# Tiles 2 to 6 and their attention played from one written list, three quarters of tile 6's first layer by 7 block products

## The chip, the core and the metric

One core of a Trainium2 chip. TensorE (PE) multiplies and writes into PSUM, which this kernel uses as 8 banks of 512 float32 in each of 128 partitions. VectorE (DVE) and ScalarE (ACT) read PSUM and SBUF; GpSimd (POOL) works in SBUF; SyncE (SP) issues most DMAs. Each engine takes its own instructions in the order in which they were recorded, and waits at one whose inputs or buffers are not ready. The metric is the device time of one execution, in microseconds (us), lower is better: 273.82 us before, median of 3 runs (273.69 to 274.09).

## The reference

Linear attention on 8 batches of 8 heads, 576 positions and 64 channels, and then a two-layer network on its 4608 rows:

```python
q_s = np.exp(q - np.max(q, axis=-1, keepdims=True))
q_s = q_s / (np.sum(q_s, axis=-1, keepdims=True) + 1e-09)
k_s = np.exp(k - np.max(k, axis=2, keepdims=True))
k_s = k_s / (np.sum(k_s, axis=2, keepdims=True) + 1e-09)
kv = np.einsum('bhsd,bhse->bhde', k_s, v)
x = np.einsum('bhsd,bhde->bhse', q_s, kv)   # then (8, 576, 8, 64) -> 4608 x 512
h = x @ w_in                                # w_in 512 x 2048
g = np.maximum(0.01 * h, h)
out = g @ w_out                             # w_out 2048 x 512
```

Inputs and output are float32; the multiplications take bfloat16.

## The kernel before

The 4608 rows are 9 tiles of 512 (t = 0 to 8). A batch has 576 rows, so tile t needs batches up to the one that covers its last row: tile 3 needs batch 3, tile 7 a little of batch 7. While the network works on tile t, the attention of a later batch b is made.

**Attention of a batch.** Three loads of 1152 KB (`load_all`) bring k, q and v into a pool of 6 raw buffers (`raw_pool`, L63). For k: a tree of maxima on DVE (`k_tree`, L156), the maximum over all positions by two transposes and small reductions (`k_allmax`, L161 to L181), the subtraction (`k_sub`, L189, on DVE for batches 3 and 4, on POOL from batch 5), the exponential on ACT (`k_exp`, L197). v is cast in two halves on ACT (`v_cast`, L207). For q: maxima on DVE (`q_max`, L221), subtraction on POOL (`q_sub`, L252), exponential on ACT (`q_exp`, L260), sums and reciprocal (`q_sum`, L269, L271), normalisation (`q_norm`, L276), and a transposing DMA from SP (`q_turn`, L434). `kv` makes 72 small products (L290) into two PSUM banks, which `kd_make` (L308, L309) reads and scales on DVE. `attend_x` makes 16 products (L415) in 64-row mode into six banks and copies them to `xT` on ACT (L406).

**The network of a tile.** First layer: for each of 16 blocks of 128 hidden channels four matmuls of 512 columns into one bank (`layer1`, L469), then the activation on ACT into `gj` (`leaky`, L478). Tiles 0 to 2 have a plain second layer (L494). Tiles 3 to 6 make the second layer by 7 products instead of 8 on 2 x 2 blocks (`seven`, L813), as Strassen and Winograd do, with differences of `gj` blocks on DVE (`gsums`, L773) and sums of `w_out` blocks (`wsums`, L695). Tiles 7 and 8 (`woven`) have both layers by 7 block products, in an order written out as a list of words (`WEAVE`): the first layer is L944, with sums of `w_in` blocks (`fsums`, L875), sums of `xT` blocks (`xsums`, L892), copies to `part` buffers on ACT (L1007) and additions on DVE (L986).

PSUM is two pools: 6 banks (`psB`) for first-layer results, `pkv`, `po` and others, and 2 banks (`psO`) for second-layer results. A tile takes the bank that was given back first. `g_pool` has 5 buffers, of which a tile of rows takes 4; `osb_pool` has 3 for output rows.

**What sets the order.** For tiles 1 to 6 a loop runs over the first layer's 16 blocks and then over the second layer's products, and after step u of tile t it calls what was hooked there by `at(t, u, ...)`: `plan3`, `plan4` and `plan(b)` hook the attention of batches 3 to 7 (L616 to L658), L607 to L610 the loads, L714 the sums 3 and 4 of `w_out`, L1046 to L1050 the sums of `w_in` and of tile 7's `xT`. At the end of tile 1, for instance, `k_allmax(3)` and its two subtractions stand at step 30, ahead of the copy of that tile's last result (L488), which stands at step 31.

Of the kernel before, what the change touches and what calls it, by code (L numbers as in the profile page):

```python
# [8 lines left out]
FP32 = mybir.dt.float32  # L9
# [10 lines left out]
L = 64  # L20
# [5 lines left out]
def kernel(  # L26
# [110 lines left out]
    def k_begin(b):  # L137
        st[b]["ke"] = ke_pool.tile([P, R, HL, D], BF16, name="ke")
        st[b]["kmax"] = mx_pool.tile([P, HL, D], FP32, name="kmax")
        st[b]["kmaxT"] = mx_pool.tile([P, HL * D], FP32, name="kmaxT")  # L140
        st[b]["kall"] = mx_pool.tile([P, HL, D], FP32, name="kall")

# [295 lines left out]

    def attend_x(b, parts, engs):

        qX = st[b]["qX"].rearrange("c (r g) (h l) -> c g h r l", g=2, h=2)
        made = []
        for i in parts:
            rs = XR[i]
            n = (rs.stop - rs.start) * L
            cols = slice(b % 4 * S + rs.start * L, b % 4 * S + rs.stop * L)
            per = 512 // n
            for g0 in range(0, 2, per):
                ps = [psB_pool.tile([P, per, n], FP32, name="po", tag=BANK_TAG) for _ in range(2)]
                for gg in range(g0, g0 + per):  # L450
                    quads(
                        b,
                        gg,
                        [p[:, gg - g0] for p in ps],
                        lambda hh: qX[:, gg, hh, rs],
                        lambda o: o.rearrange("p (r l) -> p r l", l=L),
                    )
                for hp in range(2):
                    c = 2 * g0 + hp
                    made.append((xT[:, c : c + 2 * per - 1 : 2, cols], ps[hp]))  # L460
        for i, (o, p) in enumerate(made):
            move(engs[i % len(engs)], o, p)
# [146 lines left out]
    for b in range(5, B):  # L609
        at(b - 3, 20, lambda b=b: load_all(b))  # L610

    def begin_batch(b):
        k_begin(b)
        q_begin(b)

    def plan3():  # L616
        b, t = 3, 1
        at(t, 27, lambda: begin_batch(b), lambda: k_tree(b, ALLH))
        at(t, 30, lambda: k_allmax(b), lambda: k_sub(nc.vector, b, H0), lambda: k_sub(nc.vector, b, H1))
        at(t, 26, lambda: v_cast(nc.scalar, b, 0), lambda: v_cast(nc.scalar, b, 1))  # L620
        at(t, 34, lambda: q_max(b, ALLR), lambda: q_sub(nc.gpsimd, b, ALLR))
        at(t, 37, lambda: k_exp(b, ALLH))
        at(t, 45, lambda: q_exp(b, ALLR))
        at(t, 46, lambda: q_sum(b, ALLR))
        at(t, 48, lambda: q_norm(b, ALLR))
        at(t, 49, lambda: q_turn(b))
        at(t, 52, lambda: kv(b))
        at(t, 53, lambda: kd_make(b))
        at(t, 59, lambda: attend_x(b, (0, 1), (nc.scalar,)))

    def plan4():
        b, t = 4, 2
        at(t, 5, lambda: begin_batch(b), lambda: q_max(b, ALLR), lambda: q_sub(nc.gpsimd, b, ALLR))
        at(t, 17, lambda: k_tree(b, ALLH))
        at(t, 23, lambda: q_exp(b, ALLR))
        at(t, 22, lambda: k_allmax(b), lambda: k_sub(nc.vector, b, H0), lambda: k_sub(nc.vector, b, H1))
        at(t, 21, lambda: v_cast(nc.scalar, b, 0), lambda: v_cast(nc.scalar, b, 1))
        at(t, 28, lambda: q_sum(b, ALLR), lambda: k_exp(b, ALLH))
        at(t, 31, lambda: q_norm(b, ALLR))
        at(t, 31, lambda: q_turn(b))  # L640
        at(t, 34, lambda: kv(b), lambda: kd_make(b))
        hooks[t + 1, "x"] = [lambda: attend_x(b, (0, 1), (nc.scalar,))]

    def plan(b):
        t = b - 2
        at(t, 2 if b == 5 else 0, lambda: begin_batch(b), lambda: k_tree(b, ALLH))
        at(t, 16, lambda: k_allmax(b), lambda: k_sub(nc.gpsimd, b, ALLH))
        at(t, 20, lambda: q_max(b, ALLR), lambda: q_sub(nc.gpsimd, b, ALLR))
        at(t, 18, lambda: v_cast(nc.scalar, b, 0))
        at(t, 20, lambda: v_cast(nc.scalar, b, 1))  # L650
        at(t, 26, lambda: k_exp(b, ALLH))
        at(t, 32, lambda: q_exp(b, ALLR))
        at(t, 34, lambda: q_sum(b, ALLR))
        at(t, 36, lambda: q_norm(b, ALLR))
        at(t, 38, lambda: q_turn(b))
        at(t, 42, lambda: kv(b))
        at(t, 43, lambda: kd_make(b))
        hooks[t + 1, "x"] = [lambda: attend_x(b, (0, 1), (nc.scalar,))]  # L658
# [20 lines left out]
    plan4()  # L679
    for b in range(5, B):  # L680
        plan(b)
# [32 lines left out]
    at(3, 4, lambda: wsums(3), lambda: wsums(4))  # L714
# [48 lines left out]
    SEVEN, WOVEN = 3, 7  # L763
    gsum = {}

    def gsums(g_sb, kk):
        g = g_sb[kk]
        a1, a2 = g[:, 0, :, 0 : TT // 2], g[:, 0, :, TT // 2 : TT]
        b1, b2 = g[:, 1, :, 0 : TT // 2], g[:, 1, :, TT // 2 : TT]
        n = [sum_pool.tile([P, 2, TT // 2], BF16, name=f"gs{i}{kk}") for i in range(1, 5)]  # L770
        gsum[kk] = n
        for o, x, y in ((n[0], a2, b2), (n[2], a2, a1), (n[1], a1, n[0]), (n[3], b1, n[1])):
            nc.vector.tensor_tensor(out=o, in0=x, in1=y, op=ALU.subtract)  # L773

# [14 lines left out]

    def seven(t, g_sb):  # L790
        half = lambda h, c: lambda k: g_sb[k // 2][:, h, k % 2, c * HT : (c + 1) * HT]
        gs = lambda i: lambda k: gsum[k // 2][i - 1][:, k % 2]
        w = lambda h, o: w_out_sb[:, h * NK : (h + 1) * NK, o * HO : (o + 1) * HO]
        osb = [osb_pool.tile([P, 2, O], FP32, name="out_sb") for _ in range(2)]
        acc, keep = {}, {}

        def product(u, subs, x, n):
            lhs, rhs = {
                1: (half(0, 0), w(0, 0)),
                2: (half(1, 0), w(1, 0)),  # L800
                3: (gs(4), w(1, 1)),
                4: (half(1, 1), wsum[4]),
                5: (gs(1), wsum[1]),
                6: (gs(2), wsum[2]),
                7: (gs(3), w(0, 1)),
            }[n]
            first = n in (1, 2, 5)
            for i, sub in enumerate(subs):
                if first and i == 0:
                    pool, tag = (psB_pool, BANK_TAG) if x == "Y" else (psO_pool, "pout")  # L810
                    acc[x] = pool.tile([P, 2, HO], FP32, name="acc", tag=tag)
                for k in range(NK):
                    nc.tensor.matmul(  # L813
                        acc[x][:, sub],
                        lhsT=lhs(k)[:, sub * P : (sub + 1) * P],
                        rhs=rhs[:, k],
                        start=(first and k == 0 and sub == 0),
                        stop=(k == NK - 1),
                        skip_group_check=not first or sub > 0,
                    )  # L820
                run(t, u + i)

        def save(x, i):
            keep[i] = keep_tile(i)
            nc.scalar.copy(out=keep[i], in_=acc[x])  # L825

        def add(c, os, x, i):
            nc.vector.tensor_tensor(out=osb[c][:, :, os], in0=acc[x], in1=keep[i], op=ALU.add)  # L828

        def take(c, os, x):  # L830
            nc.scalar.copy(out=osb[c][:, :, os], in_=acc[x])

        product(16, both, "X", 1)
        save("X", 1)
        product(18, both, "Y", 2)
        add(0, low, "Y", 1)
        product(20, both, "X", 6)
        save("X", 6)
        run(t, "x")
        product(22, both, "Z", 5)  # L840
        save("Z", 5)
        product(24, both, "X", 7)
        add(1, high, "X", 5)
        product(26, both, "Z", 3)
        add(0, high, "Z", 6)
        put(t, osb, 0, whole)
        product(28, both, "X", 4)
        take(1, low, "X")
        put(t, osb, 1, whole)
        run(t, 30)  # L850
        run(t, 31)
# [29 lines left out]
    def xsums(t):  # L881
        home = spare_tile("xs", [P, NT - WOVEN, 4, 2, HT], BF16)
        X = {n: home[:, t - WOVEN, n - 1] for n in range(1, 5)}
        spare["X", t] = X
        B11, B12, B21, B22 = (xblock(t, c, h) for c in both for h in both)
        for o, x, y, op in (
            (X[1], B12, B11, ALU.subtract),
            (X[2], X[1], B22, ALU.add),
            (X[3], B22, B12, ALU.add),
            (X[4], B21, X[2], ALU.subtract),  # L890
        ):
            nc.vector.tensor_tensor(out=o, in0=x, in1=y, op=op)  # L892

    WEAVE = """
# [157 lines left out]
    for t in range(1, NT):  # L1052
        if t >= WOVEN:
            woven(t)
            if t == WOVEN:
                xsums(t + 1)
# [55 lines left out]
```

## Time and profile before

| what | value |
|---|---|
| median of 3 runs | 273.82 us (273.69 to 274.09) |
| the profiled execution | 273.67 us, its span 271.9 us |
| k, q, v loads of 1152 KB by SP: median from issue to landing | 6.3, 8.5, 11.1 us |
| the transposing DMA: median from issue to landing | 4.6 us |
| `gj` from a bank of 512 columns on ACT | 603 ns, 96 times |
| `gj` from a `part` buffer, copy to one, on ACT | 627, 588 ns |
| sum of bank and `part`, difference of `gj` blocks, sum of `xT` blocks, on DVE | 687, 412 to 422, 417 ns |
| k subtraction, q subtraction on POOL | 5080, 4053 ns |

The span begins with the first instruction and ends with the last; the time around it is start and end of the execution. Rows of the profile give a group's mean time for one instruction. "Busy" on PE is modelled from the starts of pipelined matmuls; the distance from one matmul's start to the next is the better measure of its rate, and a stretch of the chain of waits, divided by its number of matmuls, gives that.

### The profile page before, as it was taken

To read this page: it belongs to the slowest core of one execution; us is meant where nothing else is said; L and a number is where in the kernel's file an instruction comes from. 1 tells how busy PE (TensorE), PEld (TensorE's weight loads), DVE (VectorE), ACT (ScalarE), POOL (GpSimd) and SP (SyncE) were. 2 spreads that over 40 slices of the span, in tenths; PEclk is the share of its full clock that TensorE was granted. 3 is DMA by queue.
4 is the path that set the end of the run, shared out by engine and by line. 5 is a ranking of instruction groups with operands and counts; after the bars stand their busy time and mean duration, and the time that the engine had idled before them with its cause. 6 is when DMAs were issued, how large, how long until landed. Compare 5 with 4: busy or idle time off the path is not lost.

```text
span 271.9 us, 5971 instructions
## 1 busy us (share of the span) xinstructions
PE 262.5 (97%) x2426; PEld 174.6 (64%) x2426; DVE 214.8 (79%) x376; ACT 178.3 (66%) x315; POOL 62.9 (23%) x46
## 2 busy tenths in 40 slices
PE   8699999999999999999999999999999999999992
PEld 3267744454444444448888884478447888888882
DVE  2997888896898499999699759974499569769952
ACT  4977790578469748767685669667863479628930
POOL 2584351009004700002900290019100000000000
PEclk9999999999999999999999999999999999999999
DMA  7999996999999039999153956310622060033004
GB/s 243 336 212 368 302 199 106 381 318 389 193 244 398 29 70 300 379 208 397 43 137 75 324 214 157 62 27 0 158 50 39 1 146 11 2 79 78 0 2 154
DMA packets 37899, 46.46 MB, mean 171 GB/s; under 512 B 18160, under 2 KB 21232, under 8 KB 37872
## 3 DMA queue, kind: packets, MB, share of 16 engines
q1 hardware_dynamic: 33504, 37.82, 47.7%
q0 software_dynamic: 4048, 7.73, 12.1%
q10 hardware_dynamic: 320, 0.52, 0.6%
q8 instruction: 19, 0.31, 0.5%
q14 instruction: 8, 0.07, 0.1%
HBM read 36.70 MB, written 9.44 MB: 170 GB/s over the span
## 4 chain that ended last, share of the span: by engine, by line
PE 88%; DMA 5%; DVE 1%; issue 0%; POOL 0%; POOLq 0%
PE ph L469 34%; PE acc L813 18%; PE pout L494 14%; PE acc L965 9%; PE ph L944 9%; DMA w_in_sb<-in_moe_w_in_dram 3%; PE po L415 2%; PE pkv L290 2%; DMA qX<-qe 2%; DVE k_raw L357 1%; POOL w_in_sb L129 0%; DVE out_sb L988 0%; POOL gate L553 0%; POOLq L553 0%
## 5 line engine op out<-in xcount | busy, mean ns | idle before, releaser
L469 PE MATMUL ph<-xT,w_in_sb 128*128 128x512 bf16 (+3 forms) x576 | 99.8, 332 | 0.3 <-DMA w_in_sb<-in_moe_w_in_dram 0.3
L478 ACT ACTIVATE gj<-ph 128x512 bf16<-128x512 f32 (+2 forms) x128 | 69.9, 575 | 24.5 <-PE ph L469 21.4
L469 PEld LDWEIGHTS <-w_in_sb 128*128 128x128 bf16 x576 | 55.7, 98 | 41.1 <-issue 0.9
L494 PE MATMUL pout<-w_out_sb,gj 128*128 128x512 bf16 x192 | 43.3, 379 | 0.0
L252 POOL TENSOR_TENSOR q_raw<-q_raw,qmax 128x2304 f32<-128x2304 f32 (+3 forms) x10 | 29.7, 2975 | 40.3 <-DVE qmax L221 40.3
L494 PEld LDWEIGHTS <-gj 128*128 128x128 bf16 x192 | 18.1, 98 | 21.8 <-issue 1.1
L189 POOL TENSOR_TENSOR k_raw<-k_raw,kall 128x2304 f32<-128x2304 f32 x3 | 15.2, 5080 | 70.9 <-ACT vb L207 36.8
L269 DVE TENSOR_REDUCE qsum<-qe 128x36 f32<-128x2304 bf16 (+4 forms) x11 | 19.7, 1795 | 12.6 <-ACT qe L260 12.5
L813 PEld LDWEIGHTS <-gs 128*128 128x128 bf16 x256 | 24.7, 98 | 3.6 <-issue 0.8
L406 ACT CAST xT<-po 128x320 bf16<-128x320 f32 (+2 forms) x45 | 17.8, 493 | 10.9 <-PE po L415 10.9
L276 DVE TENSOR_TENSOR qe<-qe,qrec 128x2304 bf16<-128x2304 bf16 (+4 forms) x12 | 21.9, 1823 | 0.3
L221 DVE TENSOR_REDUCE qmax<-q_raw 128x36 f32<-128x2304 f32 (+4 forms) x11 | 19.6, 1790 | 1.6 <-DMA q_raw<-in_q_dram 1.6
L813 PEld LDWEIGHTS <-gj 128*128 128x128 bf16 x192 | 18.8, 98 | 2.8
L197 ACT ACTIVATE ke<-k_raw 128x2304 bf16<-128x2304 f32 (+2 forms) x11 | 17.6, 1600 | 3.9 <-POOL k_raw L189 3.8
L260 ACT ACTIVATE qe<-q_raw 128x2304 bf16<-128x2304 f32 (+4 forms) x11 | 16.7, 1518 | 3.9 <-DMA qX<-qe 3.1
L986 DVE TENSOR_TENSOR part_spare<-ph,part_spare 128x512 f32<-128x512 f32 x24 | 16.0, 687 | 3.4 <-PE ph L944 3.2
L1007 ACT COPY part_spare<-ph 128x512 f32<-128x512 f32 x24 | 13.1, 588 | 7.9 <-PE ph L944 7.6
L828 DVE TENSOR_TENSOR out_sb<-acc,keep 128x512 f32<-128x512 f32 x12 | 8.2, 681 | 12.1 <-ACT keep L825 7.1
L207 ACT CAST vb<-v_raw 128x1152 bf16<-128x1152 f32 x13 | 14.5, 1151 | 1.4 <-PE pkv L290 0.8
L813 PE MATMUL acc<-wsum,gs 128*128 128x256 bf16 x128 | 15.3, 273 | 0.0
L813 PE MATMUL acc<-w_out_sb,gj 128*128 128x256 bf16 x128 | 14.6, 273 | 0.0
L813 PE MATMUL acc<-w_out_sb,gs 128*128 128x256 bf16 x128 | 14.6, 273 | 0.0
(97 smaller groups left out, 347.0 us busy)
## 6 DMA issues: line engine op xcount, KB each, us to landing
out_dram<-out_sb SPq DMA_DIRECT2D x68, 128.0 KB, 2.4
k_raw<-in_k_dram SPq DMA_DIRECT2D x6, 1152.0 KB, 6.3
q_raw<-in_q_dram SPq DMA_DIRECT2D x6, 1152.0 KB, 8.5
v_raw<-in_v_dram SPq DMA_DIRECT2D x6, 1152.0 KB, 11.1
w_in_sb<-in_moe_w_in_dram POOLq DMA_DIRECT2D x4, 512.0 KB, 7.8
w_out_sb<-in_moe_w_out_dram POOLq DMA_DIRECT2D x3, 512.0 KB, 16.0
k_raw<-in_k_dram SPq DMA_DIRECT2D x2, 576.0 KB, 5.5
v_raw<-in_v_dram SPq DMA_DIRECT2D x2, 576.0 KB, 7.5
```

Of the source, the lines that this page charges most:

```text
L197: nc.scalar.activation(out=st[b]["ke"][:, :, hs].rearrange("p r h d -> p h r d"), in_=st[b]["k"][:, hs], func=AF.Exp,)
L221: nc.vector.tensor_reduce(out=m, in_=st[b]["q"][:, :, rs], axis=AX.X, op=ALU.max)
L252: eng.tensor_tensor(out=qs, in0=qs, in1=st[b]["qmax", rs.start].unsqueeze(3).to_broadcast([P, HL, n, D]), op=ALU.subtract,)
L269: nc.vector.reduce_sum(out=qsum, in_=st[b]["qe"][:, rs], axis=AX.X)
L276: nc.vector.tensor_tensor(out=qes, in0=qes, in1=st[b]["qrec", rs.start].unsqueeze(3).to_broadcast([P, n, HL, D]), op=ALU.mult,)
L406: eng.copy(out=o, in_=i)
L469: nc.tensor.matmul(ph[:, n0:n1], lhsT=w_in_sb[:, i, j * P : (j + 1) * P], rhs=xT[:, i, (c0 + n0) % NX : (c0 + n0) % NX + n1 - n0], start=( ...
L478: nc.scalar.activation(out=o, in_=ph, func=AF.Prelu, alpha=LEAKY_SLOPE)
L494: nc.tensor.matmul(pout, lhsT=g_at(g_sb, j, tsub * P, (tsub + 1) * P), rhs=w_out_sb[:, j], start=first, stop=last,)
L813: nc.tensor.matmul(acc[x][:, sub], lhsT=lhs(k)[:, sub * P : (sub + 1) * P], rhs=rhs[:, k], start=(first and k == 0 and sub == 0), stop=(k ...
L944: nc.tensor.matmul(bank[x, p][:, jj], lhsT=lhs(k, 2 * p + jj), rhs=rhs[:, k], start=(first and k == 0 and jj == 0), stop=(k == 1), skip_gr ...
L965: nc.tensor.matmul(o, lhsT=lhs(k)[:, sub * P : (sub + 1) * P], rhs=rhs[:, k], start=(first and k == 0 and (sub == 0 or x == "Z")), stop=(k ...
```

## The change

One list of words, `SCORE`, takes the place of the loop for tiles 2 to 6, of the hooks of batches 3 (from the maxima on) to 7, and of `seven` and `gsums`. Each word is recorded in the order in which it stands. A word with a digit ahead belongs to that tile: `u14` is the first layer of block 8 x 1 + 4, `l14` its activation, `P23` the fourth quarter of the plain second layer's rows 2, `P701` half 1 of block product 7 on rows 0, `n0_1` a difference of `gj` blocks, `q`, `d` and `w` the copies, the additions and the stores of results, `m7_0` block product 7 of the first layer for quarter 0, `s` and `c` its copies to and additions into `part` buffers. Others belong to a batch: `lk lq lv` loads, `kt5.0` the first step of the tree of maxima, `km ks ke` the maximum over all, the subtraction, the exponential of k, `va vb` the casts, `qm qs qe qu qn qt` the chain of q, `kv kd` the same, `A` attention products, `x` their copies. `F` is a sum of `w_in` blocks, `X` of `xT`, `T` of `w_out`; `Z` gives buffers free.

Tile 6's quarters 0 to 2 of the first layer are 21 words `m`, and quarter 3 four words `u` (blocks 6, 7, 14, 15). `F1`, `F2` and `F3` stand in tile 2's second layer, `F4` where tile 6 begins. In the built program the two buffers of the `w_in` sums are the raw buffers of v and k of batch 3, kept to the end; the loads of batches 5 to 7 go through the other four. `k_begin` no longer claims the buffer of the exponential (`k_room` does, at `ke`). Loads are single words, no longer three together. Tiles 7 and 8 keep `WEAVE`.

```diff
-    for b in range(5, B):
-        at(b - 3, 20, lambda b=b: load_all(b))
...
     def plan3():
         b, t = 3, 1
-        at(t, 27, lambda: begin_batch(b), lambda: k_tree(b, ALLH))
-        at(t, 30, lambda: k_allmax(b), lambda: k_sub(nc.vector, b, H0), lambda: k_sub(nc.vector, b, H1))
+        at(t, 27, lambda: k_begin(b), lambda: k_tree(b, ALLH))
         at(t, 26, lambda: v_cast(nc.scalar, b, 0), lambda: v_cast(nc.scalar, b, 1))
-        at(t, 34, lambda: q_max(b, ALLR), lambda: q_sub(nc.gpsimd, b, ALLR))
...
-    at(3, 4, lambda: wsums(3), lambda: wsums(4))
...
+    SCORE = """
+        2u14 km3 ks3 2u04 2l04 2u05 2l05 2u06 2u02 2l14 2l06 2u00 ksB3 ke3 2l00 2u01 2u10 2u03 2l02 2l01
+        2l03 2u11 qm3 2l11 qs3 qm4 kt4.0 qs4 kv3 kd3 2u07 2l10 2P00 2u12 qe3 qu3 qn3 2l12 T4 kt4.1 2u13 2l13
+        2u16 2l07 2l16 2u15 2l15 2u17 2l17 2P01 kt4.2 qt3 2P02 2P03 2d0 2P10 va4 F1 kt4.3 km4 ks4 F2 ksB4 F3
+        2P11 2P12 2P13 2d1 2P20 2P21 2P22 qe4 2P23 A3.0 x3.01 A3.1 A3.2 x3.00 lk5 x3.20 qu4 qn4 2P30 x3.21
+        2P31 2P32 2P33 2d2 2d3 2w0 x3.10 x3.11 kt5.0 3u00 3u11 3u10 3l00 3u04 ke4 3u01 lq5 kt5.1 3l04 3u06
...
+        3n1_1 3P100 3P101 3n3_1 lv5 3u17 3l17 3n0_3 3n1_3 3P110 3P111 3q1 A4.0 A4.1 A4.2 va5 lq6 vb5 3P500
+        x4.00 3P501 3P510 x4.01 3n3_3 3n3_2 3P600 3P601 3P511 3q5 3P610 3P611 km5 3n2_2 qm5 3P200 3P201
+        3P210 ks5 3q6 3P700 3P211 3P701 3P710 3P300 x4.11 3P301 x4.20 3d11 3P711 3d22 3P310 x4.10 qm6 2w1
+        qs5 3P311 kt6.0 x4.21 4u06 4l06 ke5 3d12 3w0 lk7 3P400 3P401 kt6.1 3P410 3P411 4u11 3q21 kt6.2 qe5
+        qu5 4u00 4l00 4l11 qn5 4u02 4l02 4u01 lv6 4l01 4u04 qt5 4l04 4u15 4u07 4u03 4l03 4u10 4l15 4l07
+        4n2_3 4n2_1 4u14 4l14 kv5 4u16 4l10 4n0_0 kd5 4u05 4l05 kt6.3 4n2_2 4u17 4l17 4u13 4u12 4P100 4n0_2
...
+        ks7 ke7 5P301 5P310 5P311 6u06 vb7 5P400 qs7 qe7 5d12 6m2_1 X6.0 Z0 6m1_0 5P401 Z1 X6.1 X6.2 X6.3
+        6m1_1 6s1_0 F4 5P410 5P411 5q21 6s1_1 6m5_2 6m1_2 6m6_0 6m5_1 qu7 6m2_0 6l06 6m6_1 6c11_0 Z2 6m5_0
+        6s1_2 6m6_2 6s6_0 6m7_0 6s5_1 6s5_0 6m3_1 6m3_0 6s6_2 6c11_1 6c22_0 6m2_2 6m4_0 6s6_1 6m7_1 6c12_0
...
+        6n3_2 A7.0 A7.1 6P300 6P301 6q6 6n2_1 x7.10 6P700 6d11 6P701 6P710 x7.11 6P711 6P310 6P311 6d22
+        x7.01 6d12 x7.00 A7.2 x7.20 6P400 x7.21 X7.0 X7.1 X7.2 6P401 6P410 6w0 6P411 6q21 6w1 5w0 X7.3
+    """.split()
...
+    def of_tile(t, word):
+        kind, p = word.split("_")[0], int(word[-1])
+        k0 = word[0]
...
+        if k0 == "u":
+            j = int(word[1]) * NK + p
+            bank["U", t, j] = psB_pool.tile([P, TT], FP32, name="ph", tag=BANK_TAG)
+            layer1(j, bank["U", t, j], t * TT, TT)
+        elif k0 == "l" and "_" not in word:
+            h = int(word[1])
+            leaky(g_of(t, p // 2)[:, h, p % 2, 0:TT], bank["U", t, h * NK + p])
+        elif k0 == "m":
+            ahead(t, int(kind[1]), p)
+        elif k0 == "P" and len(word) == 3:
...
+        elif k0 == "P":
+            behind(t, *(int(c) for c in word[1:]))
+        elif k0 == "s":
+            nc.scalar.copy(out=fill(t, kind, p), in_=bank["Z" if kind == "s5" else "X", t, p])
...
+    def of_batch(word):
...
+        elif kind in ("ks", "ksB"):
+            if b in KS_DVE:
+                k_sub(nc.vector, b, H0 if kind == "ks" else H1)
+            else:
+                k_sub(nc.gpsimd, b, ALLH)
+        elif kind == "ke":
+            if "ke" not in st[b]:
+                k_room(b)
+            k_exp(b, ALLH)
...
+    play(SCORE)
+    play(WEAVE, 7)
+    xsums(8)
+    play(WEAVE, 8)
```

`KS_DVE` is (3, 4). `ahead`, `behind` and the rest of `of_tile` hold what `woven` and `seven` held, with the tile as an argument; for tile 6, `l11` is an activation on ACT as in the plain first layer, not the DVE form of tiles 7 and 8.

More of the change, by code (lines that the diff above doesn't have):

```diff
@@ L141, in k_begin, with k_room @@
         st[b]["kall"] = mx_pool.tile([P, HL, D], FP32, name="kall")
+    def k_room(b):
+        st[b]["ke"] = ke_pool.tile([P, R, HL, D], BF16, name="ke")
     def k_tree(b, hs, steps=slice(0, 4)):
@@ L761 @@
     ORDER = [h * NK + k for k in range(NK) for h in range(2)]
[L763 to L773, printed above, removed]
+    WOVEN, KS_DVE = 7, (3, 4)
     HT = TT // 2
@@ L788, in put @@
                 )
[L790 to L851, printed above, removed]
     spare = {}
@@ new lines, with g_of, corner @@
+    """.split()
+    gt, nt, ot, bank, slots, free, made = {}, {}, {}, {}, {}, [], {}
+    SUB = {"n0": ("a2", "b2"), "n1": ("a1", "n0"), "n2": ("a2", "a1"), "n3": ("b1", "n1")}
+    CORNER = {"a1": (0, 0), "a2": (0, 1), "b1": (1, 0), "b2": (1, 1)}
+    def g_of(t, p):
+        if (t, p) not in gt:
+            gt[t, p] = g_tile()
+        return gt[t, p]
+    def corner(t, p, z):
+        if z[0] == "n":
+            return nt[t, p, int(z[1])]
+        i, h = CORNER[z]
+        return g_of(t, p)[:, i, :, h * HT : (h + 1) * HT]
@@ new lines, in behind @@
+    def behind(t, n, sub, half):
+        G = lambda z: lambda k: corner(t, k // 2, z)[:, k % 2]
+        w = lambda h, o: w_out_sb[:, h * NK : (h + 1) * NK, o * HO : (o + 1) * HO]
+        lhs, rhs, x = {
+            1: (G("a1"), w(0, 0), "X"),
+            2: (G("b1"), w(1, 0), "Y"),
+            3: (G("n3"), w(1, 1), "Z"),
+            4: (G("b2"), wsum[4], "V" if t >= WOVEN else "X"),
+            5: (G("n0"), wsum[1], "Z"),
+            6: (G("n1"), wsum[2], "X"),
+            7: (G("n2"), w(0, 1), "X"),
+        }[n]
+        apart = x == "Z" and t >= WOVEN
+        first = n in (1, 2, 5) or x == "V"
+        if first and half == 0 and (sub == 0 or apart):
+            pool, tag = (psO_pool, "pout") if x == "X" or (x == "Z" and sub == 0) else (psB_pool, BANK_TAG)
+            b = pool.tile([P, 1 if apart else 2, HO], FP32, name="acc", tag=tag)
+            for i in [sub] if apart else both:
+                bank[x, t, "out", i] = b, 0 if apart else i
+        b, at_ = bank[x, t, "out", sub]
+        for k in range(half * NK // 2, (half + 1) * NK // 2):
+            nc.tensor.matmul(
+                b[:, at_],
+                lhsT=lhs(k)[:, sub * P : (sub + 1) * P],
+                rhs=rhs[:, k],
+                start=(first and k == 0 and at_ == 0),
+                stop=(k % (NK // 2) == NK // 2 - 1),
+                skip_group_check=not first or half > 0 or at_ > 0,
+            )
```

437 lines of the change are left out of this document (204 added, 233 removed).

## The prediction

> **What bounds the kernel now.** I read the engines' busy times first, then the chain of waits, then the stages, and last the timeline where tile 2 begins. Times are places on the span of 271.9 us; the execution around it took 273.67 us, 1.77 us more, and the sum below is made against that. Of the runs shown the median is 273.82 and the spread 0.40, so the profiled execution is an ordinary one.
>
> ```profile
> PE 262.5 (97%) x2426; PEld 174.6 (64%) x2426; DVE 214.8 (79%) x376; ACT 178.3 (66%) x315; POOL 62.9 (23%) x46
> ...
> PEclk9999999999999999999999999999999999999999
> ```
>
> PE is busy for 97% at the full granted clock. The chain that ended last shows whether that is work or waiting:
>
> ```profile
> 98.49 4.61 DMA qX<-qe
> 103.10 0.04 issue
> ...
> 190.59 9.50 PE ph L469 x44
> 200.09 0.71 PE pkv L290 x72
> 200.79 4.42 PE ph L469 x20
> 205.22 5.24 PE acc L813 x48
> 210.46 0.61 PE po L415 x16
> 211.07 7.09 PE acc L813 x64
> 218.16 9.61 PE ph L944 x88
> ```
>
> Tile 6 (190.59 to 218.16) is PE end to end: 64 matmuls of 512 columns in 9.50 + 4.42 = 13.92 us (218 ns each), 112 of 256 columns in 5.24 + 7.09 us, and in tile 7's first layer 88 in 9.61 us, 109.2 ns each, with no gap. Between tile 2 and tile 7 the chain leaves PE once for more than 0.04 us, for the transposed q of batch 3 (98.49 to 103.14), and there the gap on PE is only 0.27 us, since other products ran meanwhile. So a new order can win little: this 0.27 us, and the columns that are taken away. It can lose as much as other engines make PE wait. Their load by tiles (2, 5 and 6):
>
> ```profile
> 77.70:107.10 29.40, 29.30 (x217) 13.56 (x216) 23.55 (x34) 20.34 (x30) 8.05 (x2) 1.00 0.63 197
> ...
> 162.90:190.50 27.60, 27.60 (x267) 18.14 (x265) 21.79 (x39) 19.80 (x30) 9.11 (x3) 1.00 0.28 61
> 190.50:218.10 27.60, 27.60 (x266) 18.08 (x265) 19.75 (x34) 15.56 (x27) 0.84 (x1) 1.00 0.28 61
> ```
>
> After PE and PEld come DVE, ACT and POOL: DVE has some 6 us free in each tile.
>
> **What the change takes away on PE.** Three quarters of tile 6's first layer are 48 matmuls of 512 columns, 48 x 218 = 10.46 us. They become 7 x 3 words of 4 matmuls of 256 columns, 84 x 109.2 = 9.17 us. Gain 1.3 us, all on the path. The gap of 0.27 us goes if the transpose is in time (below: it is). Batch 7's attention is visited twice instead of once; each change to 64-row matmuls and back shows about 0.1 us on PE, so +0.2, and 0.1 comes back in tile 3's attention, where such a visit was 0.1 longer than the others. Floor with no new wait: 273.67 - 1.3 - 0.27 + 0.1 = 272.2.
>
> **What it adds elsewhere in tile 6.** DVE: 9 sums (687 ns) and 4 of xT (417 ns), 7.9 us, less the three w_in sums moved to tile 2 (3 x 1217 ns): +4.2 on 19.75. ACT: 9 copies (588) and 12 activations (627) for 12 activations (603): +5.6 on 15.56. Both stay under the 26.3 us that PE needs: hidden, if the order is right. In tile 2 the three sums make DVE 23.55 + 3.65 = 27.2 of 29.4.
>
> **Where the new order makes PE wait: the start of tile 2.** The new list starts only after tile 1's last copy, and with it batch 3's column maxima (km3), which before stood ahead of that copy:
>
> ```profile
> 77.03 0.45 DVE L161 STREAM_TRANSPOSE kmaxT<-kmax 128x256 f32<-128x256 f32 x1
> ...
> 79.33 2.63 DVE L189 TENSOR_TENSOR k_raw<-k_raw,kall 128x1152 f32<-128x1152 f32 x2
> ...
> 81.88 0.69 DVE L488 COPY out_sb<-pout 128x512 f32<-128x512 f32 x1
> 82.48 2.54 DVE L221 TENSOR_REDUCE qmax<-q_raw 128x36 f32<-128x2304 f32 x1
> 83.74 2.12 ACT L197 ACTIVATE ke<-k_raw 128x2304 bf16<-128x2304 f32 x1
> 85.11 8.05 POOL L252 TENSOR_TENSOR q_raw<-q_raw,qmax 128x2304 f32<-128x2304 f32 x2 [17.14 <-DVE qmax L221]
> 86.19 2.55 DVE L221 TENSOR_REDUCE qmax<-q_raw 128x36 f32<-128x2304 f32 x1 [1.16 <-DMA q_raw<-in_q_dram]
> ```
>
> I walk it. The copy runs at 78.05 to 78.7 (its product ends at 77.9), km3 2.3 us to 80.95, both subtractions to 83.55. ke3 starts then, no earlier than before, but in the new list only 4 activations of tile 2 stand before it, not 6; ACT is idle from 82.4 and l00, l02, l01, l03, l11, l10 wait behind ke3. It ends at 85.7; they end from 86.2 in steps of 0.545 (six took 3.27 behind ke before), l02 at 86.75, l10 at 88.95. PE (first matmul 77.73, ten u words) wants kv3 at 86.7, whose second bank is that of l02: 0.1 late. 2P00 needs l10 at 88.7: 0.3 more.
>
> Then kd3. It holds two banks, and the built program lets 2u16 begin only when its first product is written. It stands behind qm3 (83.5 to 86.0), qm4 (86.2, with its load, to 88.7) and the first maximum of batch 4 (kt4.0), which runs into POOL:
>
> ```profile
> 36.78 1.90 POOL L252 TENSOR_TENSOR q_raw<-q_raw,qmax 128x1024 f32<-128x1024 f32 x1 [3.70 <-DVE qmax L221]
> 38.63 1.66 POOL L710 COPY gj<-gj 128x256 bf16<-128x256 bf16 x1
> ...
> 132.32 4.05 POOL L252 TENSOR_TENSOR q_raw<-q_raw,qmax 128x2304 f32<-128x2304 f32 x1
> 133.57 0.69 DVE L828 TENSOR_TENSOR out_sb<-acc,keep 128x512 f32<-128x512 f32 x1 [1.00 <-PE acc L813]
> 134.18 3.28 DVE L156 TENSOR_TENSOR t<-k_raw 128x1024 f32<-128x1024 f32 x1
> ```
>
> The last row is kt5.0, 1.22 us when alone. It ended at 137.46, 1.08 us after POOL's subtraction (136.37), while the addition out of PSUM kept its 0.69. So a DVE operation with both inputs in SBUF waits until POOL's is done. POOL's q subtraction of batch 3 runs from 86.1 to 90.15; kt4.0 ends at 91.2, kd3's first product at 91.65. 2u16 would have begun at 90.9 without any wait: PE is 0.7 us late there, the 0.4 from above included.
>
> The Trainium skill says the same in "SBUF — State Buffer", section "Who interferes with whom": such a DVE instruction contends with a GpSimd one that reads SBUF, and the second to issue blocks until the first is done. The trace agrees (3.28 for 1.22 us). The rule does not say who is next when POOL has another subtraction queued, as here; if POOL were, it would be rival three.
>
> **After that**, with PE 0.7 late. The transpose of batch 3: its POOL part ends at 90.15, exp 92.3, sum 95.3, norm 97.9 (the second subtraction, pushed to 95.25 by kt4.0, is just done), landing 4.6 us on, 102.5; A3 is due at 103.7, so 0.27 is saved. From there DVE is in one long queue to kd5: column maxima 3 x 2.3, subtractions 4 x 1.3, q maxima 4 x 2.54, two trees of 2.8 and 2.4 of a third, q sums 3 x 2.93, norms 3 x 2.55, five weight sums 6.1, two copies 1.35, 19 differences of 0.39, three additions 2.05, kd 2.3: 66 us on 78.7 is 144.7, plus 1.4 at kt4.0, 1.45 for kt6.0 behind POOL and 1 for data, about 148.3. PE wants kd5's bank for 4u13 at 147.9 + 0.7 = 148.6. This fits by 0.3 us, by my count; I put it at nothing, and each us more on DVE costs about one. In tile 6, exp(q7) ends ACT's detour at 192.8; six copies of 0.56 follow, and 6m7_0 has its copy at 196.6 for 196.7; the sum c22_0, sixth in DVE's line behind q's sum of batch 7, comes at 198.7, where 6m4_0 is due at 198.4: 0.3. Tail, tiles 7 and 8, stores: as before. **Sum: 272.2 + 0.7 + 0.3 = 273.2 us**, 0.2% under 273.82. Bounds of the new waits: 0 if ke3's and kd3's detours are covered, and the rivals' figures.
>
> **The rivals.**
> *No new wait.* For it: the list of tiles 7 and 8 is of the same kind and runs without a gap (88 matmuls at 109.2 ns). Against: no attention work stands in that list. 272.2 us.
> *Late loads: slower.* The w_in sums take two of the six raw buffers from tile 2 on, so each load of batches 5 to 7 waits for the last reader of one of four. v5 is issued at about 118.1, behind a transpose and k6; its cast is due on ACT at 125.2, and q6 waits for that cast. A load landed 8.5 us after issue when three ran together (the row for q): v5 at 126.6, casts to 128.8, the first attention copy at 129.25 for 3P200, due at 128.6: 0.65. q6 then lands at 137.4 for 133.9, less 1.45 which kt6.0 no longer waits for POOL: DVE 2.1 late at kd5, 0.75 more on PE, 0.7 at 4P500. 273.2 + 2.1 = 275.3; it decides from a landing of v5 after 126. Against: a lone 1152 KB at the 398 GB/s of the fullest slice takes 3 us, and k6 with v5 6 us. The longer row (11.1 us) would give about 278.
> *POOL goes first.* If the second q subtraction (90.15 to 94.2) gets in ahead of kt4.0, this ends at 95.25, kd3 at 95.7, and 2u16 waits 4.8 instead of 0.7: 277.3. Against: at 38.63 a POOL copy (usually 0.4) queued behind a subtraction took 1.66, letting the waiting DVE norm pass.
> *The saving is given back in tile 6.* If exp(q7) is 1 us later (its chain is DVE maxima, 5.08 and 4.05 on POOL, then ACT), copies s1 to s6 are too, and every block product waits: 0.9 us, 274.1.
> *It doesn't do what it says.* F1 to F3 stand in tile 2, F4 at tile 6, not in 4 and 5; for the time that is the load above, no other case.
>
> **How the numbers follow.** A change under 0.2% (0.55 us) can't be told from none here. Forecast, new waits of 0.6 to 1.6 us: 272.8 to 273.8, chance 0.42. No new wait or nearly: 0.23 (272.1 to 272.8). Late loads or a late DVE queue: 0.20. Tile 6: 0.10. POOL first: 0.05. Below 273.27 lie all of the second and half of the first: 0.45. Within 0.2% the rest of the first but a little, and some of tile 6: 0.24. Slower 0.31. Range 272.0 to 275.3 leaves out the longer landing and POOL first; the likeliest case's own is 272.8 to 273.8.
>
> **What would show it.** PE: gaps before kv3, 2P00 and 2u16 summing to 0.7; 48 matmuls of 512 columns fewer and 84 of 256 more in tile 6, which then lasts about 26.5 us. DVE: kt4.0 of 2.5 us ending 1.08 after POOL's first q subtraction; no idle time to kd5. ACT: idle before ke3, no wait for v5. Wrong if A3 still waits for its transpose, if PE waits in tile 3 or 4 for DVE or a load by over 0.5 us, or if block products in tile 6 come slower than 109 ns.

## The result, and the profile after

The changed kernel takes 275.53 us (median of 6 runs, 274.90 to 276.17) where the kernel before takes 273.83 us beside it (6 runs, 273.6 to 274.1). The ratio is 1.006, with a 95% interval of 1.0043 to 1.0078: slower by 0.6%, where 0.2% faster was forecast. The profiled execution took 274.90 us, its span 273.1 us.

First the page's busy times and the granted clock of the kernel after:

```profile
PE 262.0 (96%) x2462; PEld 178.1 (65%) x2462; DVE 221.6 (81%) x389; ACT 179.9 (66%) x324; POOL 64.1 (23%) x46
...
PEclk9999999999999999999999999999999999999999
```

PE has 36 matmuls more (48 of 512 columns became 84 of 256) and is busy 0.5 us less, yet the span is 1.2 us longer: PE waits more. DVE has 6.8 us more work. What PE waited for is in the view of the waits (engine and line, what it waited for, us in total, times, longest), of the kernel after:

```profile
PE acc L902 <- ACT xT L410: 1.5, 1, 1.5
PE pout L324 <- POOL zero L105: 1.3, 1, 1.3
PE po L419 <- DMA qX<-qe: 1.3, 1, 1.3
```

The middle row is at the start of the kernel and was there before (1.3 us as well). The other two are new. Measured from one matmul's start to the next, less the 0.11 us of one matmul, they are 1.62 us at 127.6 (word `3P200`) and 1.42 us at 152.7 (word `A5.0`), 3.04 us together; no other gap after 77 us is over 0.25 us. The chain that ended last (start, length, what) goes through both:

```profile
115.09 1.57 ACT gj L483 x3
116.67 1.05 ACT vb L211
117.71 0.02 issue
117.73 8.93 DMA v_raw<-in_v_dram
126.66 0.02 issue
...
126.74 2.21 ACT vb L211 x2
128.95 0.33 ACT xT L410
129.28 0.04 issue
129.32 5.40 PE acc L902 x48
...
146.08 0.32 PE pkv L294 x25
146.40 7.73 DMA qX<-qe
154.12 0.14 issue
154.26 0.68 PE po L419 x16
154.94 10.59 PE acc L902 x96
```

Before, the chain between tiles 2 and 7 stayed on PE but for one transpose. Now it leaves PE twice, from 115.07 to 129.32 and from 146.40 to 154.26. The first time: ACT casts the second half of batch 4's v, which frees the raw buffer that batch 5's v is loaded into; the load takes 8.93 us; ACT casts both halves, and only then the attention copies into `xT` that stand behind the casts and that give back the bank for `3P200`. The second time: the transpose of batch 5's q, 7.73 us from issue to landing where the median before is 4.6.

Why so long shows in SP's timeline (start, length, line, operation). The kernel after:

```profile
142.09 0.54 SPq L83 DMA_DIRECT2D k_raw<-in_k_dram  x1
142.74 0.50 SPq L83 DMA_DIRECT2D v_raw<-in_v_dram  x1
146.40 5.73 SPq L438 DMA_TRANSPOSE qX<-qe  x1
```

and the kernel before:

```profile
146.00 2.82 SPq L434 DMA_TRANSPOSE qX<-qe  x1
148.86 0.58 SPq L83 DMA_DIRECT2D k_raw<-in_k_dram  x1
149.54 0.48 SPq L83 DMA_DIRECT2D q_raw<-in_q_dram  x1
150.12 0.45 SPq L83 DMA_DIRECT2D v_raw<-in_v_dram  x1
```

The transpose is issued 0.4 us later than before, but two loads of 1152 KB now stand ahead of it, where the three loads stood behind. The packets in the trace, started per us, tell them apart: 2304 bytes for a load, 256 for the transpose (2304 of them); stores are left out:

```
us              143  144  145  146  147  148  149  150  151  152  153
after, loads     33  135  166  178  177  180  150    3    2    0    0
after, transp.    0    0    0    0    0    0   94  411   56 1132  611
before, transp.   0    0    0    0  625  848  793   38    0    0    0
```

The transpose's first packet starts at 149.67, while the loads' last ones are still starting: 3.3 us after its issue, where it was 1.2 before. Its packets then take 4.0 us instead of 3.0; the small number in us 151 is part of that, and no run here shows why.

### The profile page after: what moved, and what is told of

The parts are those of the page before. It is cut to its first block, busy times and chain, and to the rows that moved or that the text cites. A ratio compares the mean times of both kernels' runs of the same rounds, so it can differ in the third digit from the quotient of the medians.

```text
span 273.1 us, 6059 instructions
## 1 busy us (share of the span) xinstructions
PE 262.0 (96%) x2462; PEld 178.1 (65%) x2462; DVE 221.6 (81%) x389; ACT 179.9 (66%) x324; POOL 64.1 (23%) x46
## 3 DMA queue, kind: packets, MB, share of 16 engines
q0 software_dynamic: 4048, 7.73, 12.0%
## 4 chain that ended last, share of the span: by engine, by line
PE 80%; DMA 11%; ACT 2%; DVE 1%; issue 0%; POOL 0%; ACTq 0%; POOLq 0%
PE ph L474 26%; PE acc L902 25%; PE pout L499 14%; PE ph L872 12%; DMA qX<-qe 5%; DMA v_raw<-in_v_dram 3%; DMA w_in_sb<-in_moe_w_in_dram 3%; PE po L419 2%; ACT vb L211 1%; PE pkv L294 1%; DVE k_raw L361 1%; ACT gj L483 1%; POOL w_in_sb L129 0%; DVE out_sb L851 0%; ACT xT L410 0%
## 5 line engine op out<-in xcount | busy, mean ns | idle before, releaser
L474 PE MATMUL ph<-xT,w_in_sb 128*128 128x512 bf16 (+3 forms) x528 | 89.9, 327 | 0.3 <-DMA w_in_sb<-in_moe_w_in_dram 0.2
L483 ACT ACTIVATE gj<-ph 128x512 bf16<-128x512 f32 (+2 forms) x119 | 62.5, 574 | 23.6 <-PE ph L474 20.0
L902 PEld LDWEIGHTS <-gs 128*128 128x128 bf16 x384 | 37.2, 98 | 5.3 <-issue 0.8
L499 PEld LDWEIGHTS <-gj 128*128 128x128 bf16 x192 | 18.1, 98 | 22.3 <-issue 1.1
L902 PEld LDWEIGHTS <-gj 128*128 128x128 bf16 x288 | 27.9, 98 | 5.7 <-issue 1.8
L851 DVE TENSOR_TENSOR out_sb<-acc,keep 128x512 f32<-128x512 f32 (+1 forms) x20 | 12.6, 636 | 16.5 <-PE acc L902 7.2
L902 PE MATMUL acc<-w_out_sb,gj 128*128 128x256 bf16 x192 | 24.4, 273 | 1.5 <-ACT xT L410 1.5
L902 PE MATMUL acc<-w_out_sb,gs 128*128 128x256 bf16 x192 | 22.8, 273 | 0.0
L902 PE MATMUL acc<-wsum,gs 128*128 128x256 bf16 x192 | 22.6, 273 | 0.0
L953 DVE TENSOR_TENSOR gs<-gj 128x512 bf16<-128x512 bf16 x48 | 19.0, 419 | 2.1 <-ACT gj L483 2.0
L953 DVE TENSOR_TENSOR gs<-gj,gs 128x512 bf16<-128x512 bf16 x48 | 19.5, 420 | 0.7
```

The costliest lines, as they stand in the source:

```text
L474: nc.tensor.matmul(ph[:, n0:n1], lhsT=w_in_sb[:, i, j * P : (j + 1) * P], rhs=xT[:, i, (c0 + n0) % NX : (c0 + n0) % NX + n1 - n0], start=( ...
L483: nc.scalar.activation(out=o, in_=ph, func=AF.Prelu, alpha=LEAKY_SLOPE)
L499: nc.tensor.matmul(pout, lhsT=g_at(g_sb, j, tsub * P, (tsub + 1) * P), rhs=w_out_sb[:, j], start=first, stop=last,)
L851: nc.vector.tensor_tensor(out=o, in0=x, in1=y, op=ALU.add)
L902: nc.tensor.matmul(b[:, at_], lhsT=lhs(k)[:, sub * P : (sub + 1) * P], rhs=rhs[:, k], start=(first and k == 0 and at_ == 0), stop=(k % (NK ...
L953: nc.vector.tensor_tensor(out=nt[t, p, i], in0=x, in1=y, op=ALU.subtract)
```

## The experiments

For each kernel the tables and texts below give, besides the median, the length of tiles 2 to 6 in the profiled execution: from the first matmul of tile 2 to the first of tile 7. It is 140.27 us before and 142.00 after.

**The two waits, one at a time.** Theory A at this point: batch 5's v comes late because it is queued behind batch 6's k, and batch 5's transpose because batch 7's k is ahead of it. First the changed kernel once more, as the base:

> The changed kernel as it is, for the comparison on one chip. Expected 275 to 276 us, 1.2 to 2.2 above the kernel before, with two gaps on PE: some 1.6 us in tile 3 (at 3P200, behind the casts of v5) and 1.4 in tile 4 (at A5, behind the transpose of batch 5's q).

Measured 275.75 us (275.27 to 277.51), ratio 1.007 [1.005, 1.009]. The profiled run, 277.51 us, had a gap of 2.82 us at `3P200` instead of 1.62, so this gap differs from execution to execution of one kernel. With it came something that the other profile had not shown: 3.41 us at a granted clock of 0.5. The last group of experiments is about that.

```diff
-  3l16 lk6 3u12
+  3l16 lv5 3u12
...
-  3n3_1 lv5 3u17
+  3n3_1 lk6 3u17
```

> lk6 and lv5 change places on SP's queue; v5 gets the buffer that k4 left, k6 that of v4. Theory A (v5 is late because its data come behind k6's on one queue): v5 lands about 3 us sooner, at 123 to 124 instead of 126.7, the 1.6 us gap at 3P200 goes, the gap at A5 stays, 1.6 us less than the changed kernel. Theory B (v5 is late because of the four buffers, that is because it waits for the cast of v4): the cast ended at 117.7, when SP was at this load anyway; 0.3 us less at most.

Measured 274.12 us, ratio 1.0024 [1.0006, 1.0042]; tiles 2 to 6 141.01. Issued at 117.08, ahead of k6, v5 lands in 6.8 us; the casts start at 124.38 instead of 126.74, and the gap at `3P200` is gone. The other is there, 2.04 us; PE's waits have it, by the modelled end of the matmul ahead, as

```profile
PE po L419 <- DMA qX<-qe: 1.9, 1, 1.9
```

```diff
-  3w0 lk7 3P400
+  3w0 3P400
...
-  4u04 qt5 4l04
+  4u04 qt5 lk7 4l04
```

> lk7 moves from before to behind qt5, so that only v6 is ahead of the transpose of batch 5's q. Theory A (the transpose's data wait behind two loads, landing 7.7 us after issue): landing falls to about 4.6 us, the gap of 1.4 us at A5 goes, the one at 3P200 stays; 1.4 us less than the changed kernel. Rival C (the transpose is late because qn5 is, in DVE's long queue): its issue stays at 146.4, and the gap shrinks by 0.5 us at most.

Measured 274.26 us, ratio 1.0016 [1.0, 1.0033]; tiles 2 to 6 141.22. The transpose lands 5.4 us after its issue (which came at 147.57, behind the longer gap of tile 3) and the gap at `A5.0` is gone. The one at `3P200` is left, 2.17 us; in PE's waits:

```profile
PE acc L902 <- ACT xT L410: 2.0, 1, 2.0
```

Moving one of the two loads was enough.

**Both.**

> Both SyncE swaps at once: batch 5's v ahead of batch 6's k, and batch 5's transpose ahead of batch 7's k. Theory A (two waits of 1.6 and 1.4 us for late data, and nothing else, separate the changed kernel from the forecast's floor): both gaps vanish; 275.6 - 1.6 - 1.4 = 272.6 us, faster than the kernel before by some 0.45%, and no stretch of half clock. Theory B (the written list is tight in general; DVE or ACT is the next limit and opens other gaps when these close): about 273.5 to 274, at least one new gap of 0.5 us or more before tile 7.

Measured 272.10 us (271.85 to 272.58) against 273.92 us, ratio 0.9939 [0.9927, 0.9951]: faster than both kernels, 1.3% below the changed one. Tiles 2 to 6 take 139.06 us. No gap of over 0.25 us is left there. The chain that ended last of this kernel at the two places:

```profile
124.83 8.84 PE acc L902 x80
...
145.73 4.47 PE ph L474 x40
150.20 1.75 PE acc L902 x16
151.95 0.61 PE po L419 x16
152.56 10.59 PE acc L902 x96
```

PE runs through `3P200`, inside the first row, and from tile 4's first layer over batch 5's attention (L419) into the second-layer products without a stop. Theory B, that another engine takes over, is refuted: in tiles 2 to 6 the two waits were what separated the change from its floor. The profiled difference there, 142.00 - 139.06 = 2.94 us, is the 3.04 us of the two gaps but for 0.1. The medians differ by 3.4 us; the profiled execution of the changed kernel was its fastest, and the gap at `3P200` can be longer, as above, but the other runs have no profile.

**What the block products of tile 6 are worth.** In the kernel with both swaps the words `6m`, `6s`, `6c`, tile 6's `l11` to `l22` and `X6` are replaced by twelve `u` and twelve `l`; the `w_in` sums stay.

```diff
-  6m2_1 X6.0 Z0 6m1_0
+  6u00 Z0 6u01 6l00
...
-  6m6_0 6m5_1 qu7 6m2_0 6l06 6m6_1 6c11_0
+  6l10 qu7 6u02 6l11 6l06 6u03 6l02
...
```

> As the kernel with both swaps, but tile 6's first layer is made plainly (64 matmuls of 512 columns, 16 activations), without the 21 block-product words, their copies, their sums and the sums of xT; the w_in sums stay where they are, since tiles 7 and 8 need them. Theory A (the block products save their PE time and all that they add on DVE and ACT is hidden): 1.3 us slower than the kernel with both swaps, about 273.9. Rival (the additions on DVE and ACT give part of it back): under 0.8 us slower.

Measured 274.35 us (273.56 to 274.64), 2.25 us above the kernel with both swaps. Tiles 2 to 6 take 140.25 us, 1.19 more than with the block products and within 0.02 of the kernel before: in these tiles the written list alone neither wins nor loses, and the block products are the whole gain, 1.19 us where 1.3 was reckoned. The 2.25 us between the medians are more than was expected. In the profiles 0.7 us of it lie outside these tiles (0.2 before tile 2, 0.5 after the last product); what causes that, and the rest, is not settled.

**Why v5 is late: the sums, the four buffers, or the queue.** Batch 4's transpose is issued at 114.07 in the changed kernel, and k6 and v5 stand behind it on SP. It waits for the normalisation on DVE, ahead of which the three `w_in` sums had been put. A first experiment moved these sums to tile 5, which also leaves six raw buffers for the loads until then:

```diff
-  va4 F1 kt4.3 km4 ks4 F2 ksB4 F3
+  va4 kt4.3 km4 ks4 ksB4
...
-  4q21 4w1 5u16 5l17 5P500
+  4q21 4w1 5u16 5l17 5P500 F1 F2 F3
```

> F1, F2 and F3 move from tile 2 to the end of tile 5's first layer, so the loads of batches 5 to 7 have all six raw buffers and DVE has 3.65 us less in tile 2. SP's order stays. Theory A (place on SP's queue): v5 is issued behind the transpose and k6 as before, 0.3 us sooner, q6 now runs with it; the gap at 3P200 stays at 1.2 to 2, time within 0.5 us of the changed kernel. Theory B (four buffers): the gap at 3P200 goes, 1.6 us less. If DVE's queue had been the cause of the second gap, it goes here, 1.4 us less.

Measured 277.74 us (277.09 to 278.13), ratio 1.0138 [1.0118, 1.0158]; tiles 2 to 6 144.35 us. The gap at `3P200` went, and that at `A5.0` stayed (1.70 us). The loss is a new wait in tile 5, 2.18 us, and a stretch of half clock behind it (the last group below); the timeline of DVE in this kernel (start, length, line, operation, tiles) and its waits show it:

```profile
177.71 1.22 DVE L756 TENSOR_TENSOR fs_spare<-w_in_sb 128x2048 bf16<-128x2048 bf16 x1
178.97 1.23 DVE L756 TENSOR_TENSOR fs_spare<-w_in_sb,fs_spare 128x2048 bf16<-128x2048 bf16 x1
180.11 1.22 DVE L756 TENSOR_TENSOR fs_spare<-w_in_sb 128x2048 bf16<-128x2048 bf16 x1
181.25 0.88 DVE L953 TENSOR_TENSOR gs<-gj,gs 128x512 bf16<-128x512 bf16 x2
```

```profile
PE acc L902 <- DVE gs L953: 2.0, 1, 2.0
```

The differences of `gj` blocks that PE needs next stand behind 3.6 us of sums. This kernel could not tell the sums from the buffers, since it changed both. The next moves the sums by less, from the k work of batch 4 to behind the normalisation of q: the same four buffers, the same DVE work, the transpose early.

```diff
-  va4 F1 kt4.3 km4 ks4 F2 ksB4 F3
+  va4 kt4.3 km4 ks4 ksB4
...
-  2P33 2d2 2d3 2w0
+  2P33 2d2 2d3 F1 F2 F3 2w0
```

> The changed kernel with the three w_in sums F1 to F3 moved from the k work of batch 4 to behind the normalisation of q of batch 4, same number of DVE operations and same four buffers. Theory A2 (v5 is late because the sums hold up that normalisation on DVE, its transpose is then issued some 3 us later and the loads of k6 and v5 stand behind it in SyncE's queue): the transpose of batch 4 issued at about 111, v5's load at about 115, landing near 124, no gap before 3P200; the gap of 1.4 to 2 us at batch 5's attention stays; about 274.1 us. Rival (four buffers instead of six make v5 late: its buffer comes free only at 117): v5 is issued at 117.5 as before, the gap of 1.6 us stays, 275.6 us.

Measured 274.22 us, ratio 1.002 [1.0007, 1.0034]; tiles 2 to 6 140.94. SP's timeline in this kernel:

```profile
111.26 2.87 SPq L438 DMA_TRANSPOSE qX<-qe  x1
114.22 0.53 SPq L83 DMA_DIRECT2D k_raw<-in_k_dram  x1
118.21 0.37 SPq L83 DMA_DIRECT2D v_raw<-in_v_dram  x1
126.89 0.37 SPq L83 DMA_DIRECT2D q_raw<-in_q_dram  x1
```

Each side was right in half. The transpose and k6 come 2.8 and 2.7 us earlier, as A2 says. But v5 is issued at 118.21, not at 115: its buffer is not free before ACT has cast the second half of v4 (it starts at 117.02 and takes 1.16), as the rival says. Still the gap at `3P200` is gone and the cast starts at 124.65: issued 4 us after k6, v5 lands in 6.0 us instead of 8.9, at 124.2. So v5's issue is set by the four buffers in both kernels, 117.73 and 118.21. What makes it land at 126.66 instead of 124.2 is k6, put into the same queue 0.85 us ahead of it, and k6 is there at that time because the transpose ahead of it was late. Together with the transpose of batch 5:

> The sums behind q's normalisation and batch 5's transpose ahead of batch 7's k load. Theory A2: both gaps vanish, 272.6 us, level with the two swaps of loads. Rival (four buffers): one gap of about 1.6 to 2 us stays, 274.2 us.

Measured 272.46 us (271.92 to 272.70), ratio 0.9947 [0.9934, 0.996]; tiles 2 to 6 139.06, as with the two swaps of loads. A third of a microsecond between the two medians is not told apart by these intervals.

**What a gap on PE costs.** The gap of 2.82 us in the second profile of the changed kernel, and the one of 2.18 us in tile 5 of the kernel with late sums, were followed by matmuls of 256 columns at 213 ns from start to start instead of 109. To see whether the gap does this, the kernel with both swaps got a gap of known size at `3P200`: the cast of the second half of v5 once, twice and three times more.

```diff
-  va5 lq6 vb5 3P500
+  va5 lq6 vb5 vb5 vb5 vb5 3P500
```

> The kernel with both swaps, and the second half of batch 5's v cast on ScalarE once more (1.1 us of extra work ahead of the copies for which 3P200 waits; the result is the same). It makes a gap of known size on TensorE where the changed kernel had one: about 1.0 us. Theory G (a gap costs its own length, and from somewhere near 2 us on also a stretch of 3.4 us at half clock, about 1.7 us more): no half clock, 273.1 to 273.3 us. Rival (gaps cost their own length only; the half clock of two earlier profiles has another cause): the same here.

> The cast twice more: a gap of about 2.1 us. Theory G: near the threshold, so some runs near 274.3 and some 1.7 us higher, with a granted clock of 0.99 instead of 1.0 in those. Rival: all runs near 274.3 us with a clock of 1.0.

> The cast three times more: a gap of about 3.2 us. Theory G: all or nearly all runs with a half-clock stretch, 272.1 + 3.2 + 1.7 = 277.0 us, and in the profile matmuls of 256 columns at 213 ns for 3.4 us after the gap. Rival: 275.3 us, matmuls at 109 ns after the gap. The first condition of the Trainium skill's TensorE: Matmul & The Clock Gate, Part 1 (half rate after an idle window of about 3.4 us) would speak for the rival here.

| extra casts | gap in the profile | median us (runs) | tiles 2 to 6 | mean clock of the runs |
|---|---|---|---|---|
| 0 | none | 272.10 (5) | 139.06 | 0.996 to 1.0 |
| 1 | none | 272.56 (6) | 139.30 | 0.995 to 1.0 |
| 2 | 1.42 us | 273.86 (10) | 140.48 | 0.996 to 1.0 |
| 3 | 2.61 us | 276.75 (4) | 143.33 | 0.993 to 0.994 |

The gaps are shorter than expected, since ACT had some 0.8 us to spare: the first cast costs nearly nothing. From two casts to three the gap grows by 1.19 us and tiles 2 to 6 by 2.85. The difference of 1.66 us is seen in the windows (stretch, its length, PE busy, PEld busy, DVE, ACT and POOL busy, granted clock, DMA share, GB/s) of the kernel with three casts, right behind the gap:

```profile
130.90:134.40 3.50, 3.50 (x19) 2.58 (x19) 0.00 (x0) 2.89 (x7) 3.50 (x2) 0.56 0.77 219
134.40:138.00 3.60, 3.60 (x33) 3.16 (x32) 1.50 (x3) 0.00 (x0) 2.74 (x1) 0.96 0.79 268
```

and of the kernel with two:

```profile
129.50:133.00 3.50, 3.50 (x33) 3.13 (x33) 1.65 (x2) 2.89 (x7) 3.50 (x2) 1.00 0.73 215
```

19 matmuls in 3.5 us against 33, at a clock of 0.56 against 1.00. Theory G holds in that a long gap costs more than its length, and the rival (its own length only) falls. Only one run of each kernel was profiled, but the mean clocks agree: of the ten runs with two casts none is out of line, all four with three are.

## Why the prediction was wrong, point by point

*The floor (272.2 us) was right for tiles 2 to 6; that the whole time fits it so closely is partly luck.* Two kernels that keep the change and take away its two waits run in 272.10 and 272.46 us. Their tiles 2 to 6 are 1.21 us shorter than before, and with the 0.25 us of small waits below that makes 1.46, where the floor took off 1.47. The terms were off singly: the PE saving in tile 6, 1.3 us by the sum, measured 1.19; the wait at `A3` went, but it was 0.17 us and not 0.27 (from the last product to the first of the attention 0.48 us before, 0.31 after, as at the changes where nothing waits); the attention of batch 4 in tile 3 became 0.32 us shorter (0.94 to 0.62), not 0.1; batch 7's second visit cost the 0.2. The medians of the kernel before and of the one with both swaps lie 1.8 us apart, so 0.6 us of that is outside these tiles or between executions, and no run here shows why.

*The start of tile 2 was forecast 0.7 us late and was 0.25 us late.* The small waits came at `kv3` (0.07 us) and at `2P00` (0.18). At `2u16` there was none, though DVE did about what had been walked. Here are the timelines of POOL and of DVE of the kernel after:

```profile
85.83 9.04 POOL L256 TENSOR_TENSOR q_raw<-q_raw,qmax 128x2304 f32<-128x2304 f32 x2 [18.16 <-DVE qmax L225]
```

```profile
88.33 2.63 DVE L160 TENSOR_TENSOR t<-k_raw 128x1024 f32<-128x1024 f32 x1
90.89 0.16 DVE L312 RECIPROCAL krec<-pkv 128x2 f32<-128x2 f32 x1
91.08 0.29 DVE L313 TENSOR_TENSOR kd<-pkv,krec 128x128 bf16<-128x128 f32 x1
```

The first maximum of batch 4 waited for POOL's first subtraction and took 2.63 us instead of 1.22; `kd3`'s first product was written at 91.37, where the walk had 91.65. But `2u16` began at 90.86, before that: in the trace it is `2u15`, one word later, that waits for a semaphore of DVE (its first weight load, at 91.51), and `2u15` began at 91.72, in time. So the due time was wrong by a word (0.87 us), not the walk. The maximum ended at 90.96, 1.08 us after POOL's first subtraction, as forecast; POOL's second one began in that time and took 5.04 us instead of 4.05, so that the two took 9.04 us instead of 8.05. *POOL goes first* is refuted by this.

*DVE's long queue to `kd5` was sized well.* It was to end at 148.3 (its terms add up to 148.55), with nothing lost; in the changed kernel `kd5` ends at 148.46, without a gap on PE ahead of `4u13`. With both swaps it ends at 147.41.

*Tile 6 was forecast 0.3 us late and was not late.* The rows of the windows for tiles 2 and 6 of the kernel after (by the tiles' places in the kernel before, so the last 1.5 us of tile 6 are not in the second):

```profile
77.70:107.10 29.40, 29.39 (x217) 13.29 (x215) 28.30 (x37) 19.05 (x29) 9.04 (x2) 1.00 0.65 199
...
190.50:218.10 27.60, 27.60 (x311) 22.32 (x310) 23.20 (x42) 19.94 (x37) 1.91 (x1) 1.00 0.22 42
```

PE is busy throughout; 60 matmuls of the block products take 6.55 us in the chain, 109 ns each. In tile 2 DVE does 28.3 of 29.4 us, as forecast (27.2) within 1.1. *The saving given back in tile 6* is refuted.

*The step that failed* is the one that begins "From there DVE is in one long queue to kd5" and puts what happens after tile 2 "at nothing". It followed DVE alone from 98 to 148 us. In the same stretch SP's queue had been rewritten too, and there both losses arose. The prediction's own sign of being wrong came true: PE waited in tile 3 for a load, and in tile 4 for a transpose, by over 0.5 us each. One of the two losses stood in the text as the rival *Late loads* (with a late DVE queue, a chance of 0.20): v5 was to land at 126.6 and landed at 126.66, the copy was to come at 129.25 and PE went on at 129.32. That the landing fits so well is luck: v5 was issued 0.4 us earlier than reckoned and took 8.93 us instead of the 8.5 of a row with three loads. The argument against it ("k6 with v5 6 us") took the rate of the fullest slice for the whole. The 1024 packets of k6 and v5 started from 118.10 to 126.07, 8.0 us: some 170 a us in the middle, but 42 in the first us and 29 in the last but one, and the landing came 0.6 us behind the last. Its price there, 0.65 us, became 1.62 because PE arrived at 127.7 and not at 128.6. The rest of that rival did not happen: q6 was there at 135.3, not at 137.4, and DVE lost nothing by it.

The other loss, the transpose of batch 5, is in no part of the prediction. The prediction took the median of 4.6 us from issue to landing for batch 3 and did not ask for batches 5 to 7 what is queued ahead. The median hid a case of the same kind: in the kernel before, the transpose of batch 4 landed 8.4 us after its issue, the last packets of three loads ahead of it starting until 115.8; PE did not wait for it. Its row in SP's timeline before:

```profile
113.41 4.88 SPq L434 DMA_TRANSPOSE qX<-qe  x1
```

The diff showed the new neighbours: before, each batch's three loads came at step 20 of a tile and SP reached them behind the transpose that waited there; in the list `lk7` and `lv6` stand ahead of `qt5`. That the sum of both, 275.5 us, comes close to the 275.3 of the rival is chance: half of the path is another.

*It doesn't do what it says* was no matter of time, as put: F1 to F3 cost their 3.65 us of DVE in tile 2. But where they stand did count, by the transpose behind them.

## What to carry to other kernels

When an order is rewritten, walk every queue that it reorders, the queue of the DMA issuer first: a load moved ahead of a transfer that PE waits for can hold it up (here two of them, 7.7 us from issue to landing instead of 4.6). A load's time from issue to landing depends on what was issued just ahead of it (v5 took 6.0 us with k6 4 us ahead and 8.9 with k6 0.85 us ahead), so take the row for the same neighbours or add up their packets, with the slow start and end. And when the floor of a change is computed with care and the result lies above it, look for the few waits in the chain that ended last; here two moved loads gave 3.4 us back (275.53 to 272.10).

## What the hardware showed that was not expected

A gap on PE of somewhat over 2 us can cost more than its length: 3.41 us at half clock come with it, up to 1.7 us more. Ten runs of the kernel with a gap of 1.42 us in its profile show no sign of it in their mean clock; all four of the kernel with 2.61 us do. In between the length alone does not decide: 2.17 us in one profile was followed by the full clock and 2.18 us in another by the half.

The traces' records of the granted clock show what does, in these profiles. The stretches at full clock ahead of the three stretches at half clock last 122.88, 126.29 and 177.49 us, that is 36, 37 and 52 times 3.413 us, so the clock changes at the borders of windows of this length. Counted from the start of each trace's first stretch at full clock, the longest gap of each profile lies in these windows as follows (gaps measured as above, from start to start less one matmul):

| profile | gap, us | most of it in one window, us | clock of the next window |
|---|---|---|---|
| both swaps, two casts more | 1.42 | 1.42 | 1.0 |
| changed kernel | 1.62 | 1.62 | 1.0 |
| sums behind q's normalisation | 1.98 | 1.98 | 1.0 |
| v5 ahead of k6 | 2.04 | 1.99 | 1.0 |
| transpose ahead of k7 | 2.17 | 1.26 | 1.0 |
| sums in tile 5 | 2.18 | 2.18 | 0.5 |
| both swaps, three casts more | 2.61 | 2.61 | 0.5 |
| changed kernel again | 2.82 | 2.18 | 0.5 |

So it goes by how much of the gap falls into one window, here with the limit somewhere between 1.99 and 2.18 us. Where the windows begin differs from trace to trace (4.0 to 7.2 us from the span's start), so near the limit one kernel can meet both cases. This is also the likely cause, though not shown run by run, of four single runs, at 275.9 to 276.4 us, of the three kernels that kept one of the two gaps (either swap alone, and the sums behind q's normalisation), with a mean clock of 0.992 or 0.993, where their gap was about 2 us. In the changed kernel run again the half clock began at 130.12, before the gap ended at 130.76, and part of it cost nothing.

The Trainium skill, in "TensorE: Matmul & The Clock Gate", Part 1 ("The HAM clock gate"), says that PE runs at half rate after at least one idle window of about 3.4 us and comes back after a busy one, the window being free-running. The 3.41 us at half clock agree with the window's length. The idle time does not: 2.18 us of a gap in one window were enough in two profiles, and 2.61 us in a third.

The Trainium skill also says, in "DMA: Bandwidth & Descriptors", section "Queues, rings and completion order", that each DMA engine takes the descriptors of a ring in their order. The table of packets above agrees: SP's transpose began 3 us after its issue, while the loads ahead of it were starting their last packets.
